# Windowed attention and a squared-ReLU layer: GpSimd's masks at another time, other first blocks and turns, a fourth relu tile

## The chip, the cores and the metric

The kernel runs on one core of a Trainium2 chip. The core has a matrix engine (TensorE, PE in the profile), VectorE (DVE), ScalarE (ACT), GpSimd (POOL) and SyncE (SP, which here issues the DMAs). The metric is the device time of one execution in microseconds; of several executions the median is given. A profiled execution gives the trace.

## The reference

Input are q, k and v of shape (8 batches, 8 heads, 576 positions, 64) in float32, two weights (512 x 2048 and 2048 x 512) and two scalars s and b. Output is (4608, 512) in float32.

```
scores = q @ k.T / 8, kept where |i - j| <= 32, else -1e9
attn   = softmax(scores);  x = (attn @ v), heads side by side: (4608, 512)
h = x @ w_in;  g = s * relu(h)**2 + b;  out = g @ w_out
```

## The kernel before

**Two halves on one engine.** PE does both the attention and the two weight products. A *block* is a run of tokens that goes through the first product together; the list `sizes` (L341) gives their lengths: 96, 256, 160, 256, 256 and then 512 each. The first three cover tokens 0 to 511. `s1(m, f0)` (L1108) does the first product of block m for a group of 128-wide slices of the hidden layer: four slices at once up to 128 tokens, two up to 256, one beyond (`group`, L1105). Its matmuls are L1119, into one of two halves of the PSUM tile W, taken in turn; ACT's relu (L1126) goes from there into one of NR1 tiles R1, taken in turn; DVE's square (L1128) goes into GT. `early()` (L1160) does the second product of the first 512 tokens, two slices at a time, into four PSUM banks (L1168), and DVE makes the result with s and b (L1153). `s2` (L1132) does the second product of all later tokens (L1137). For b, `colsum()` (L1176) sums w_out's columns on PE (L1182, L1189), with two helper tiles that GpSimd fills and that lie in the last two of the output tiles OUTS (L1180, L1181).

**Weights.** w_in and w_out come in four chunks of two halves each, through a ring of eight float32 tiles STG (512 KB loads, L550), and GpSimd casts each half to bf16 (L553, 128 x 1024). The loads are issued by SP in a fixed order; a load waits until its STG tile's earlier user has been cast. Batch 1's q and k pairs (256 KB loads, L662) follow w_out in the same ring.

**Attention of batches 0 and 1.** A *pair* is two heads of q or k. It is cast to bf16 (L687: for batch 1, q on GpSimd, k on DVE), and four PE transposes (L700) bring it into W, in one of the two halves in turn; ACT copies q from there (L705), DVE copies k (L706). A *turn* is q and k of one pair. `pair_scores` (L932) then does the scores (L939) and ACT the exponential (L982). In batch 0 the mask is in the scores' bank from the start (tile NEG, opened by L957); in batch 1 DVE multiplies with MASK (L987). A *unit* is 128 positions of attention output: L864 (times v), the reciprocal and the division on DVE (L888, L890), a transpose (L897), and ACT's copy into XT (L905), which the first product reads. Batch 0's units end at tokens 96, 224, 352, 480 and 576. v of batch 1 is cast by GpSimd, of later batches by DVE (L587).

**Attention of batches 2 to 7.** q and k are loaded in larger pieces (L747), cast (L755), transposed by DMAs that SP issues (L762), k is rearranged by GpSimd (L772); L783 clears margins of the q tile. Scores are L806, the exponential L834, the mask L838, with one of four tiles MASKS, of which the first is MASK.

**Masks.** `band` (L480) makes a tile with two GpSimd affine selects (L482, L487). IDENT and both halves of NEG are made at the start. `masks(after)` (L512) makes MASK's two halves, then three copies with parts cleared (L517, L520). It is called in `attention()` (L1050) with the last unit of batch 0 as `after`.

**The order of the work.** Each piece of work is added to a graph with an engine, an estimated cost, what it reads and writes, and a key. `plan()` (L127) goes through the graph with these estimates and always takes the piece that can start earliest, and of those with equal start the lowest key; that gives each engine's fixed order. `emit()` writes it with semaphore waits. An estimate decides the order alone, not the time on the chip. The order in which pieces are added matters too, as it sets the dependencies: two pieces in the same half of W follow each other as they were added. FIRST (L34) is the list by which the first three blocks' `s1` calls are added: (m, i) is block m with weight chunk i, and TURN adds one turn of batch 1. HELD (L38) is, for each chunk of w_out, the delay in ns that `plan()` assumes between its cast and its first reader. `due(c, u)` (L464) gives a unit's key from the blocks' planned times.

Of the kernel before, what the change touches and what calls it, by code (L numbers as in the profile page):

```python
# [19 lines left out]
NUNIT = (NTILE + 1) // 2  # L20
# [10 lines left out]
WINE = ("pool", "pool", "pool", "pool")  # L31
TURNKEY = -17.5
TURN = (None, 0)
FIRST = ((0, 0), (1, 0), (0, 1), (1, 1), (2, 0), (2, 1), (0, 2), (1, 2), (2, 2), TURN, (0, 3), TURN, (1, 3), TURN, (2, 3), TURN)  # L34
WOUTE = (("pool", "pool"),) * 4
TAIL = ("act", "dve")
HOST = (("k", 3), ("q", 0))
HELD = (2200.0, 1500.0, 1000.0, 1000.0)  # L38
OPEN = -24.4
REST = ("pool", "pool")  # L40
ORDER1 = (("w", 0), ("w", 1), ("w", 2), ("w", 3), ("p", 0), ("p", 1), ("p", 2), ("p", 3),
# [285 lines left out]
def bass_sliding_window_symmetric__then__act_starrelu_kernel(  # L327
# [10 lines left out]
    B = q.shape[0]  # L338
    T = B * S

    sizes = [96, 256, 160, 256, 256]  # L341
    NE = 3
    while sum(sizes) < T:
        sizes.append(min(512, T - sum(sizes)))
# [6 lines left out]
    with ExitStack() as es:  # L351
# [16 lines left out]
            uid["n"] += 1  # L368
            return es.enter_context(nc.psum_tensor(f"{nm}_{uid['n']}", list(shape), dt))

        NSTG, NNAT, NEX, NXN, NR1, NOUT, XR = 8, 6, 5, 5, 3, 5, 2048
        WIN_BF = sb((128, 4, DFF), BF16, "win")
        WOUT_BF = sb((128, 16, DM), BF16, "wout")
        XT = sb((128, NPAIR, XR), BF16, "xt")
# [14 lines left out]
        MASK = MASKS[0]  # L389
# [7 lines left out]
        ONESW = sb((128, 128), BF16, "onesw")  # L397
# [5 lines left out]
        OUTS = [sb((128, DM), F32, "outs") for _ in range(NOUT)]  # L403
# [17 lines left out]
        g = _Graph(queues)  # L421
        add = g.add
# [70 lines left out]
        band(IDENT[:, :], ONESW[:, :], "IDENT", 0, 0, -98)  # L493
        for p0 in (0, 64):
            band(NEG[p0:p0 + 64, :], NEG[p0:p0 + 64, :], ("NEG", p0), 0, 64, -97, -FAR, source=("NEG", p0))
        ones = ONESW.rearrange("p (one c) -> p one c", one=1).to_broadcast((128, 4, 128))
        add("pe", [lambda e: e.matmul(W[:, 1, :].rearrange("p (a c) -> p a c", a=4), lhsT=ONESW[:, :], rhs=ones,
                                      start=True, stop=True)] * WARM,
# [12 lines left out]

        def masks(after):  # L512

            for p0 in (0, 64):
                band(MASK[p0:p0 + 64, :], ONESW[p0:p0 + 64, :], ("MASK", 0, p0), 0, 64, -24.0, waits=[after])
            for i, cuts in ((1, ((0, 96), (64, 0))), (2, ((64, 96),)), (3, ((0, 0),))):
                add("pool", lambda e, i=i: e.tensor_copy(MASKS[i][:, :], MASK[:, :]), 250,  # L517
                    reads=[("MASK", 0, 0), ("MASK", 0, 64)], writes=[("MASK", i, 0), ("MASK", i, 64)], key=0.0)
                for p0, c0 in cuts:
                    add("pool", lambda e, i=i, p0=p0, c0=c0: e.memset(MASKS[i][p0:p0 + 64, c0:c0 + WIN], 0.0), 150,  # L520
                        writes=[("MASK", i, p0)], key=0.0)
        for i in range(2):
            for c0 in (0, WIN + S):
                zero("dve", QT[i][:, :, c0:c0 + WIN], ("QTZ", i, c0), 150, key=-98 if i == 0 else -20)
            add("dve", lambda e, i=i: e.memset(VB[:, i * NUNIT:i * NUNIT + NUNIT, :, :].rearrange("p t h c -> p (t h) c")[:, :, D:D + 1], 1.0), 150,
                writes=[("VBO", i)], key=-57 if i == 0 else -20)
# [3 lines left out]
        land = {}  # L530
# [53 lines left out]
        def cast_v(c, u, key, eng, slack):  # L584
            vs, vb, n = number(c, u) % NUNIT, number(c, u) % (2 * NUNIT), 64 * len(tiles(c, u))
            add(eng, (lambda e: e.copy(VB[0:n, vb, :, 0:D], VST[0:n, vs, :, :])) if eng == "act" else
                (lambda e: e.tensor_copy(VB[0:n, vb, :, 0:D], VST[0:n, vs, :, :])),  # L587
                {"act": 617.0, "dve": 420.0, "pool": 750.0}[eng],
                reads=[("VST", vs)], writes=[("V", vb, y) for y in (0, 1)], key=key, slack=slack)

        def load_rows(y, load_key):

# [426 lines left out]
        def attention():  # L1019
            seq = {"k": -200.0}  # L1020

            def nxt():
                seq["k"] += 1.0
                return seq["k"]

            def w(which, i):
                for x in (0, 1):
                    load_weights(which, i, x, nxt(), WINE[i] if which == "in" else WOUTE[i][x])

            for pr in range(NPAIR):  # L1030
                for name in "qk":
                    load_pair(0, name, pr, nxt())
                    turn_pair(0, name, pr, -60.0 + 0.1 * pr, banks, K0[pr] if name == "k" else Q0[pr], 200.0)
                pair_scores(0, pr)
            pick()
            for name, t in ORDER0:
                if name == "v":
                    load_tail(nxt())
                elif name == "r":
                    load_rows(t, nxt())  # L1040
                elif name == "e":
                    load_rest(0, nxt(), REST[0], -26.5, 200.0)
                else:
                    w("in", t)
            place_v()
            turn_rest(0, -23.9, banks)
            place_tail()
            last_scores(0)
            first_units()
            masks(land["av", 0, NUNIT - 1])  # L1050
            for i, src in enumerate((moe_s, moe_b)):
                add("sp", lambda e, i=i, src=src: e.dma_start(SROW[0:128:32, i:i + 1], src.partition_broadcast(4)),
                    600.0, writes=[("SROW", i)], dma=("l", 1, 15.0), key=nxt())
            add("dve", lambda e: e.stream_shuffle(SB128[:, :], SROW[:, :], [0] * 32), 150,
                reads=[("SROW", 0), ("SROW", 1)], writes=[("SB128", 0), ("SB128", 1)], key=P2[0] - 8.0, slack=500.0)
            for step in ORDER1:
                if step[0] == "w":
                    w("out", step[1])
                elif step[0] == "v":
                    load_v(1, step[1], nxt(), "sp", [land["rows", y] for y in (0, 1)])  # L1060
                    cast_v(1, step[1], due(1, 0) - 4.0 + step[1], EV1[step[1]], 800.0)
                elif step[0] == "e":
                    load_rest(1, nxt(), REST[1], due(1, 0) - 1.4, 500.0)
                else:
                    for name in "qk":
                        load_pair(1, name, step[1], nxt())
            yield S
            for pr in range(NPAIR):
                if pr:
                    yield S  # L1070
                for name in "qk":
                    turn_pair(1, name, pr, TURNKEY + 0.1 * pr, banks, "dve" if name == "k" else "pool", 500.0)
                pair_scores(1, pr)
            turn_rest(1, due(1, 0) - 1.4, banks)
            last_scores(1)
            for u in range(NUNIT):
                last.append((1, u))
                close()
                yield closed[0]
            for b in range(PAIRS, B):  # L1080
                c = seq_of(b)
                later(b, due(c, group_of(b)[0]) - 24.0)
                for i, u in enumerate(group_of(b)):
                    load_v(c, u, due(c, u) - 35.0, late(b), [paced(b, PACEV[min(b, 4) - 2][i])])
                    cast_v(c, u, due(c, u) - 4.0, EV2[i], SLACK[3])
                for u in group_of(b):
                    unit(c, u)
                    yield closed[0]
            if seq_tiles(LONG) % 2 == 0:
                unit(LONG, seq_units(LONG) - 1)  # L1090
            while last:
                close()
            yield T
# [81 lines left out]

        def colsum():  # L1176

            even, block = OUTS[NOUT - 2][:, 0:128], OUTS[NOUT - 1][:, :]
            made = [land["av", 0, NUNIT - 1]]
            add("pool", lambda e: e.memset(even, 1.0 / 32), 150, writes=[("OUTS", NOUT - 2)], key=-19.0, waits=made)  # L1180
            add("pool", lambda e: e.memset(block, 0.0), 500, writes=[("OUTS", NOUT - 1)], key=-19.0, waits=made)  # L1181
            add("pe", [lambda e, fc=fc, x=x: e.matmul(  # L1182
                SC[32 * x:32 * x + 32, 0, 0:128], lhsT=ONESW[:, 0:32], rhs=WOUT_BF[:, fc, 128 * x:128 * x + 128],
                start=(fc == 0), stop=(fc == 15)) for fc in range(16) for x in range(4)],
                1100, reads=["ONESW"] + [("Wout", i, x) for i in range(4) for x in (0, 1)], writes=[("SC", 0)], key=-12.0)
            add("dve", [lambda e, x=x: e.tensor_copy(block[32 * x:32 * x + 32, 128 * x:128 * x + 128],
                                                     SC[32 * x:32 * x + 32, 0, 0:128]) for x in range(4)],
                800, reads=[("SC", 0)], writes=[("OUTS", NOUT - 1)], key=-12.0)
            add("pe", lambda e: e.matmul(SC[:, 1, :], lhsT=even, rhs=block, start=True, stop=True),  # L1189
                950, reads=[("OUTS", NOUT - 2), ("OUTS", NOUT - 1)], writes=[("SC", 1)], key=-12.0)  # L1190
            add("dve", lambda e: e.tensor_scalar(CVEC[:, :], SC[:, 1, :], SB128[:, 1:2], None, ALU.mult),
                680, reads=[("SC", 1), ("SB128", 1)], writes=[("CVEC", x) for x in (0, 1)], key=P2[0])

        units, made = attention(), 0
# [6 lines left out]
        made = next(units)  # L1201
        colsum()
        for m, i in FIRST:
            if m is None:
                made = next(units)
# [268 lines left out]
```

## Time and profile before

| | us |
|---|---|
| median of 3 executions | 316.41 (315.55 to 317.66) |
| the profiled execution | 318.05 |
| its span, first to last instruction | 316.3 |
| PE busy | 303.9 (96%) |
| DVE, ACT, POOL busy | 194.8, 141.9, 91.7 |
| mean granted PE clock | 0.987 |

The profile's page has a row of tenths for each engine over 40 equal slices of 7.9 us: 9 means busy for 90% or more. PE's row is 9 from the eleventh slice on; the first ten have smaller digits. The row PEclk is the clock granted to PE in tenths of full speed. DMA was busy for 73% of the span; its busiest slices moved 380 to 393 GB/s, from 16 to 36 us, when the weights come in.

| stretch, us | PE busy | DVE busy | ACT busy | POOL busy | clock | GB/s |
|---|---|---|---|---|---|---|
| 0 to 20 | 15.93 | 10.75 | 11.73 | 7.73 | 0.91 | 295 |
| 20 to 40 | 17.65 | 11.30 | 9.02 | 17.64 | 1.00 | 371 |
| 40 to 60 | 18.01 | 13.54 | 9.39 | 10.46 | 0.91 | 245 |
| 60 to 72 | 11.40 | 11.54 | 4.60 | 9.65 | 1.00 | 168 |
| 80 to 100 | 20.00 | 16.22 | 9.66 | 6.97 | 1.00 | 189 |

A matmul's end is modelled, so a busy PE can still have small losses. A wait is put down to what came last.

### The profile page before, as it was taken

How to read it: one execution, taken by the hardware profiler on the slowest of the kernel's cores; microseconds unless marked ns; L12 is line 12 of the kernel's file. 1: busy time of each engine (PE TensorE's matmuls, PEld its weight loads, DVE VectorE, ACT ScalarE, POOL GpSimd, SP SyncE). 2: the span in 40 equal slices, each digit the busy share in tenths (PEclk: the TensorE clock that was granted, in tenths of full speed). 3: DMA queues.
4: the chain of work that ended last, by engine and by line, in shares of the span. 5: the costliest groups of instructions: out<-in, count | busy, mean ns of one | idle time of the engine just before them, and what ended most of it. 6: DMA issues, size and time to landing. Idle time of an engine off the chain costs nothing.

```text
span 316.3 us, 7961 instructions
## 1 busy us (share of the span) xinstructions
PE 303.9 (96%) x3348; PEld 161.6 (51%) x3348; DVE 194.8 (62%) x387; ACT 141.9 (45%) x224; POOL 91.7 (29%) x110
## 2 busy tenths in 40 slices
PE   6888969999999999999999999999999999999995
PEld 2466656567664454544444444444444444444444
DVE  4666465895897897795577576967445543333312
ACT  4746326356544775654265435444444333333300
POOL 3468973670406136131513411451000000000000
PEclk9799979999999999999999999999999999999999
DMA  6999999998994998799799799996221110000022
GB/s 214 330 380 388 360 229 241 225 188 296 248 182 137 297 166 164 242 206 153 184 290 151 149 251 313 167 169 157 64 63 51 52 46 33 35 35 33 36 96 74
DMA packets 100055, 56.10 MB, mean 177 GB/s; under 512 B 72048, under 2 KB 91248, under 8 KB 100016
## 3 DMA queue, kind: packets, MB, share of 16 engines
q1 hardware_dynamic: 100016, 55.56, 73.0%
q8 instruction: 27, 0.44, 0.6%
q14 instruction: 12, 0.10, 0.1%
HBM read 36.70 MB, written 9.44 MB: 146 GB/s over the span
## 4 chain that ended last, share of the span: by engine, by line
PE 83%; DMA 5%; POOL 4%; SPq 3%; DVE 3%; issue 1%; POOLq 0%
PE w L1119 36%; PE o L1137 35%; PE avn L864 4%; DMA stg<-in_moe_w_in_dram 4%; POOL wout L553 3%; PE sc L806 2%; DMA stg<-in_v_dram 1%; PE avn L1168 1%; SPq L662 1%; PE o L1168 1%; DVE outs L1153 1%; PE w L700 1%; PE avn L897 1%; SPq L673 1%; DVE vb L587 1%
## 5 line engine op out<-in xcount | busy, mean ns | idle before, releaser
L1119 PE MATMUL w<-xt,win 128*128 128x512 bf16 (+3 forms) x768 | 144.8, 327 | 1.1 <-issue 0.6
L1126 ACT ACTIVATE r<-w 128x512 bf16<-128x512 f32 (+2 forms) x148 | 86.6, 586 | 104.0 <-PE w L1119 87.6
L1137 PE MATMUL o<-wout,gt 128*128 128x512 bf16 (+1 forms) x528 | 126.8, 373 | 0.3 <-DVE gt L1128 0.3
L1128 DVE TENSOR_TENSOR gt<-r 128x512 bf16<-128x512 bf16 (+2 forms) x148 | 77.2, 526 | 75.9 <-ACT r L1126 75.5
L1119 PEld LDWEIGHTS w<-xt,win 128*128 128x128 bf16 x768 | 67.7, 98 | 53.9 <-issue 0.8
L1137 PEld LDWEIGHTS o<-wout,gt 128*128 128x128 bf16 x528 | 50.7, 98 | 55.8 <-DVE gt L1128 0.6
L755 POOL CAST nat<-stg 128x1024 bf16<-128x1024 f32 (+1 forms) x21 | 26.6, 1265 | 64.4 <-DMA stg<-in_q_dram 42.5
L772 POOL COPY kt<-ktr 128x512 bf16<-128x512 bf16 (+1 forms) x30 | 31.1, 1037 | 37.4 <-DMA ktr<-nat 35.9
L834 ACT ACTIVATE ex<-sc 128x1024 bf16<-128x1024 f32 (+1 forms) x28 | 28.6, 1023 | 22.5 <-PE avn L864 21.7
L1153 DVE SCALAR_TENSOR_TENSOR outs<-o,sb,cvec 128x512 f32<-128x512 f32 (+1 forms) x35 | 25.4, 728 | 11.4 <-PE o L1137 11.3
L890 DVE TENSOR_TENSOR xn<-avn,rec 128x512 bf16<-128x512 f32 (+1 forms) x31 | 21.3, 688 | 1.0 <-DVE rec L888 0.2
L838 DVE TENSOR_TENSOR ex<-ex,mask 128x1024 bf16<-128x1024 bf16 (+1 forms) x28 | 21.2, 757 | 1.1 <-ACT ex L834 0.5
L864 PE MATMUL avn<-vb,ex 64*64 64x65 bf16 x944 | 19.9, 197 | 0.3
L864 PEld LDWEIGHTS avn<-vb,ex 64*64 64x64 bf16 x944 | 12.9, 106 | 13.2 <-issue 7.8
L755 DVE CAST nat<-stg 128x1024 bf16<-128x1024 f32 (+1 forms) x15 | 12.2, 810 | 3.7 <-DMA stg<-in_k_dram 1.9
L587 DVE CAST vb<-vst 128x512 bf16<-128x512 f32 (+1 forms) x28 | 13.8, 494 | 0.8 <-DMA vst<-in_v_dram 0.7
L888 DVE RECIPROCAL rec<-avn 128x8 f32<-128x8 f32 (+1 forms) x31 | 6.2, 201 | 8.3 <-PE avn L864 8.0
L806 PE MATMUL sc<-qt,kt 64*64 64x128 bf16 x432 | 11.3, 216 | 0.0
L700 PE MATMUL w<-ident,nat 128*128 128x128 bf16 x64 | 7.0, 253 | 3.9 <-POOL nat L687 3.4
L905 ACT COPY xt<-avn 128x512 bf16<-128x512 bf16 (+2 forms) x14 | 7.1, 516 | 6.3 <-PE avn L897 6.3
L705 ACT COPY qt<-w 128x512 bf16<-128x512 bf16 x8 | 4.7, 584 | 11.3 <-PE w L700 11.3
L553 POOL CAST win<-stg 128x1024 bf16<-128x1024 f32 x8 | 8.6, 1080 | 3.6 <-DMA stg<-in_moe_w_in_dram 3.4
(119 smaller groups left out, 156.8 us busy)
## 6 DMA issues: line engine op xcount, KB each, us to landing
out_dram<-outs SPq DMA_DIRECT2D x35, 256.0 KB, 2.6
vst<-in_v_dram SPq DMA_DIRECT2D x28, 256.0 KB, 4.4
stg<-in_k_dram SPq DMA_DIRECT2D x6, 1024.0 KB, 10.6
stg<-in_q_dram SPq DMA_DIRECT2D x6, 1024.0 KB, 6.4
stg<-in_moe_w_in_dram SPq DMA_DIRECT2D x8, 512.0 KB, 9.3
stg<-in_moe_w_out_dram SPq DMA_DIRECT2D x8, 512.0 KB, 10.3
stg<-in_q_dram SPq DMA_DIRECT2D x8, 256.0 KB, 5.3
stg<-in_k_dram SPq DMA_DIRECT2D x8, 256.0 KB, 5.1
```

Source lines behind the costliest of these rows:

```text
L553: add(eng, (lambda e: e.copy(dst, stg)) if eng == "act" else (lambda e: e.tensor_copy(dst, stg)), {"act": 1040.0, "dve": 690.0, "pool": 11 ...
L755: add(eng, lambda e, x=x: e.tensor_copy(nat[0:top, 1024 * x:1024 * x + 1024].rearrange("p (i h d) -> p h i d", h=H, i=2), stg[0:top, :].re ...
L772: add("pool", lambda e, c=c, w=w: e.tensor_copy(KT[slot][:, :, c:c + w].rearrange("p a (s i) -> p a s i", i=4), KTR[slot][:, :, :, c // 4: ...
L834: add("act", lambda e, dst=flat_dst, src=flat_src: e.activation(dst, src, AF.Exp, bias=0.0, scale=0.125), 190 + 0.833 * 512 * len(hs), rea ...
L838: add("dve", lambda e, flat=flat, mask=mask: e.tensor_tensor(flat, flat, mask, ALU.mult), 130 + 0.53 * 512 * len(hs), reads=[("E", ei, hp, ...
L864: return [lambda e: e.matmul(av[64 * x:64 * x + 64, h, 0:D + 1], lhsT=buf[64 * g:64 * g + 64, h % 2, h // 2, c:c + 64], rhs=VB[64 * g:64 * ...
L890: add("dve", lambda e: e.tensor_tensor(XN[xi][0:p1, :].rearrange("p (a c) -> p a c", a=H), av[0:p1, :, 0:D], REC[ri][0:p1, :].rearrange("p ...
L1119: add("pe", [lambda e, g=g, kc=kc: e.matmul(wt[:, g, :], lhsT=WIN_BF[:, kc, (f0 + g) * 128:(f0 + g + 1) * 128], rhs=XT[:, kc, t0 % XR:t0 % ...
L1126: add("act", lambda e: e.activation(rt, wt, AF.Relu, bias=0.0, scale=1.0), 190 + 0.833 * ng * nt, reads=[("W", wb)], writes=[("R1", rb)], ...
L1128: add("dve", lambda e: e.tensor_tensor(GT[gs][:, f0:f0 + ng, g0:g0 + nt], rt, rt, ALU.mult), 130 + 0.53 * ng * nt, reads=[("R1", rb)], wri ...
L1137: add("pe", [lambda e, fc=fc: e.matmul(O[:, ob, 0:cn], lhsT=GT[gs][:, fc, g0:g0 + 128], rhs=WOUT_BF[:, fc, c0:c0 + cn], start=(fc == 0), s ...
L1153: add("dve", lambda e: e.scalar_tensor_tensor(OUTS[us][:, 0:cn], bank, SB128[:, 0:1], CVEC[:, c0:c0 + cn], ALU.mult, ALU.add), 200 + 1.07 ...
```

## The change

Six edits.

1. MASK's two halves are made at the start, behind NEG, with key -96 and no wait for batch 0's attention. The two fills for `colsum()` follow them, waiting only for the last of these selects.
2. The three copies of MASK and their clearings wait for the last V cast of batch 1 (the new entry `land["vb", 1]`).
3. The first blocks are 224, 128 and 160 tokens.
4. FIRST has another order: chunk 1 of block 0 directly behind chunk 0, chunk 3 of block 0 ahead of the first turn, and the first two turns directly behind each other.
5. HELD is 1500 for chunks 2 and 3 of w_out.
6. There are four R1 tiles instead of three.

```
-FIRST = ((0, 0), (1, 0), (0, 1), (1, 1), (2, 0), (2, 1), (0, 2), (1, 2), (2, 2), TURN, (0, 3), TURN, (1, 3), TURN, (2, 3), TURN)
+FIRST = ((0, 0), (0, 1), (1, 0), (1, 1), (2, 0), (0, 2), (2, 1), (1, 2), (2, 2), (0, 3), TURN, TURN, (1, 3), TURN, (2, 3), TURN)
-HELD = (2200.0, 1500.0, 1000.0, 1000.0)
+HELD = (2200.0, 1500.0, 1500.0, 1500.0)
...
-    sizes = [96, 256, 160, 256, 256]
+    sizes = [224, 128, 160, 256, 256]
...
-        NSTG, NNAT, NEX, NXN, NR1, NOUT, XR = 8, 6, 5, 5, 3, 5, 2048
+        NSTG, NNAT, NEX, NXN, NR1, NOUT, XR = 8, 6, 5, 5, 4, 5, 2048
...
+        for p0 in (0, 64):
+            band(MASK[p0:p0 + 64, :], ONESW[p0:p0 + 64, :], ("MASK", 0, p0), 0, 64, -96)
+        even, block = OUTS[NOUT - 2][:, 0:128], OUTS[NOUT - 1][:, :]
+        add("pool", lambda e: e.memset(even, 1.0 / 32), 150, writes=[("OUTS", NOUT - 2)], key=-95.0, waits=[g.tasks[-1]])
+        add("pool", lambda e: e.memset(block, 0.0), 500, writes=[("OUTS", NOUT - 1)], key=-95.0, waits=[g.tasks[-1]])
...
-            for p0 in (0, 64):
-                band(MASK[p0:p0 + 64, :], ONESW[p0:p0 + 64, :], ("MASK", 0, p0), 0, 64, -24.0, waits=[after])
             for i, cuts in ((1, ((0, 96), (64, 0))), (2, ((64, 96),)), (3, ((0, 0),))):
                 add("pool", lambda e, i=i: e.tensor_copy(MASKS[i][:, :], MASK[:, :]), 250,
-                    reads=[("MASK", 0, 0), ("MASK", 0, 64)], writes=[("MASK", i, 0), ("MASK", i, 64)], key=0.0)
+                    reads=[("MASK", 0, 0), ("MASK", 0, 64)], writes=[("MASK", i, 0), ("MASK", i, 64)], key=0.0, waits=[after])
...
+            land["vb", c] = g.tasks[-1]
...
-            masks(land["av", 0, NUNIT - 1])
...
+            masks(land["vb", 1])
...
-            even, block = OUTS[NOUT - 2][:, 0:128], OUTS[NOUT - 1][:, :]
-            made = [land["av", 0, NUNIT - 1]]
-            add("pool", lambda e: e.memset(even, 1.0 / 32), 150, writes=[("OUTS", NOUT - 2)], key=-19.0, waits=made)
-            add("pool", lambda e: e.memset(block, 0.0), 500, writes=[("OUTS", NOUT - 1)], key=-19.0, waits=made)
```

## The prediction

> **What bounds the kernel now.** I read the busy table, then the 40 slices, then PE's waits, then the timelines around the one large hole. PE is the bound from 76 us on: the slices show it full, and no wait of PE ends there. What this change can move lies in front, where PE holes show as digits under 9.
>
> ```profile
> PE 303.9 (96%) x3348; PEld 161.6 (51%) x3348; DVE 194.8 (62%) x387; ACT 141.9 (45%) x224; POOL 91.7 (29%) x110
> PE   6888969999999999999999999999999999999995
> POOL 3468973670406136131513411451000000000000
> PEclk9799979999999999999999999999999999999999
> ```
>
> The largest wait of PE is for POOL's cast of batch 1's first q pair (L687). Columns: total us, times, longest.
>
> ```profile
> PE w L700 <- POOL nat L687: 3.4, 2, 2.4
> PE w L497 <- DVE onesw L475: 1.1, 1, 1.1
> PE o L1168 <- POOL wout L553: 0.7, 1, 0.7
> PE w L1119 <- issue: 0.6, 1, 0.6
> ```
>
> The timelines of PE and POOL (start, length, what) show that hole and what POOL did instead.
>
> ```profile
> 38.54 1.03 PE L1168 MATMUL o<-wout,gt 128*128 128x512 bf16 x4
> 41.99 0.99 PE L700 MATMUL w<-ident,nat 128*128 128x128 bf16 x8 [2.42 <-POOL nat L687]
> 42.90 1.90 PE L1182 MATMUL sc<-wout,onesw 128*32 128x128 bf16 x64
> 44.73 0.61 PE L700 MATMUL w<-ident,nat 128*128 128x128 bf16 x4
> ...
> 37.23 1.04 POOL L553 CAST wout<-stg 128x1024 bf16<-128x1024 f32 x1
> 38.33 0.29 POOL L520 MEMSET mask<- 64x32 bf16 x2
> 38.69 1.04 POOL L553 CAST wout<-stg 128x1024 bf16<-128x1024 f32 x1
> 39.79 0.29 POOL L517 COPY mask<-mask 128x128 bf16<-128x128 bf16 x1
> 40.14 1.04 POOL L553 CAST wout<-stg 128x1024 bf16<-128x1024 f32 x1
> 41.24 0.68 POOL L687 CAST nat<-stg 128x512 bf16<-128x512 f32 x1
> ```
>
> Mask work stands between the w_out casts, the q cast comes last, and PE idles 2.42 us. The clock is granted in stretches of 3.4 us; the one after the hole is at half (columns: length, busy by engine, clock, DMA share, GB/s).
>
> ```profile
> 38.70:42.10 3.40, 0.98 (x6) 0.31 (x5) 1.25 (x1) 0.00 (x0) 3.15 (x5) 1.00 0.79 241
> 42.10:45.50 3.40, 3.40 (x81) 3.01 (x80) 1.96 (x5) 0.71 (x2) 2.27 (x6) 0.50 0.97 230
> 60.00:72.00 12.00, 11.40 (x191) 7.57 (x191) 11.54 (x21) 4.60 (x9) 9.65 (x10) 1.00 1.04 168
> ```
>
> **1. Masks made at the start.** Four band selects and two memsets move in front of POOL's first cast. The six selects already there run from 1.13 to 3.51 us, one per 0.43; so 4 x 0.43 + 0.20 + 0.52 + two gaps of 0.07 = 2.6 us, to 6.1. POOL is idle from 3.51 until 6.76 (q's landing), so 0.65 us of cover stays: cost 0. Past the cover, each us would delay batch 0's second q pair, whose transposes wait at 7.42. A select may slip in front of NEG's last one and hold PE's first opening matmuls (3.57) by 0.43; pair 1 has 1.0 us of idle PE ahead of it to absorb that.
>
> **2. POOL's casts of w_out.** Between 24.4 and 41.2 us the mask work is 0.29 + 0.35 + 0.36 + 0.29 + 0.20 + 0.52 + 0.36 + 0.29 + 0.29 = 2.95 us. Not all of it is gained, since the casts then run into their loads. The trace has the w_out landings at 29.36, 30.71, 32.01, 33.37, 36.08, 37.45 and 38.87 us (one is missing), one per 1.36, against 1.04 for a cast. The last cast starts at 40.14; it could start at 38.9, a gain of 1.2. The q pair landed at 39.57, so its cast runs from 40.0 to 40.6, and L700 can start at about 40.7 instead of 42.0. The k cast on DVE waits for a load as well (40.18) and does not move. SP issues batch 1's pairs when w_out casts free their tiles, so those issues come up to 1.2 us sooner; but these pairs land at one per 0.68 us up to 44.4, at some 380 GB/s, as much as the load stream shows anywhere, so I count nothing for them. V and batch 2's loads behind them in SP's queue may start 1 us earlier; nothing either.
>
> **3. Turns and blocks.** (0,3), two calls of 8 matmuls, now stands ahead of the first turn. Starts of successive matmuls are 43 ns apart at 96 columns, 69 at 160, 109 at 256: 0.42 ns a column and 2.5 ns. So 224 columns take 96 ns and (0,3) 1.5 us. PE leaves its last piece at 39.4 to 39.6; with (0,3) it has work until 41.0, past 40.7. The 2.42 hole closes; I leave 0.1 for the k half: **-2.3 us**. Bounds: -1.2 (only the earlier cast counts, because a piece of L1168 that stood before the turn moves behind it) and -2.42. The total of matmul columns is the same: 64 x (43 + 109 + 69) against 64 x (96 + 56 + 69) is 14.1 us both times, and 20 relu groups stay 20. Block 0 now needs unit 1's columns, copied at 19.35 to 19.94; the first group waited for a w_in cast until 20.23 anyway: 0.
>
> **4. The half clock.** With the hole gone, the stretch from 42.1 should run at full clock. Its price by rows: the 8 transposes took 0.99 us, and four take 0.22 at full (-0.55); L1182's 64 have no row at full clock (0 to -0.92); the rest is -0.1 to -0.25. Bounds 0 and -1.7 (half of 3.4); I take **-1.2**, nearest to the rows. The Trainium skill, TensorE: Matmul & The Clock Gate, What's actually happening, has the clock fall after at least one idle window of about 3.4 us; this trace shows it after 2.42 us of idle, so the measurement decides. By that rule this term would be 0 and the sum 1.7.
>
> **5. The three mask copies and four memsets** (3 x 0.29 + 4 x 0.12 with gaps, 1.8 us) follow batch 1's last V cast, which ends at 52.1. POOL then idles 3.01 us for a load of batch 2, so they cost 0. If that load came at once, they would delay batch 2's casts by 1.8; its scores start at 77.6, its first k copies are done by 70, so this is covered too. The added wait has only batch 2's casts behind it. The masks other than the first are read from batch 3 on.
>
> **6. Fourth relu tile, later due times for w_out chunks 2 and 3.** One wait of ACT for DVE is seen ahead of 75 us (0.38 at 34.17). The due times change only the order in which PE meets its work. 0, bounds -0.4 and +0.5.
>
> **7. What is late next.** DVE was busy 11.54 of 12 us from 60 to 72. Arriving 3.5 us sooner, the work of 40 to 72 (13.5 + 11.5 us) must fit into 28.5: 88%. I give back PE's own idle of that stretch, 12.0 - 11.4: **+0.6** (bounds 0 and +2.0, three result tiles of L1153 in a row). The loads for batches 3 and on are issued as PE and DVE proceed; batch 3's first k copy is done at 97.7, its scores start at 101.1: 3.4 us of slack, more than the gain.
>
> **Sum.** -2.3 - 1.2 + 0.6 = -2.9 us, from the profiled execution's 318.05 (span 316.3 and 1.75 around it) to 315.15. That execution lies 1.6 above the median of 316.41; the same difference on the median gives **313.5 us**. About 1% is what a measurement can tell from no change, so this is near the border.
>
> **Rivals.**
> - *Early stage gains too* (17%). Blocks 0 and 1 need three units instead of four, so chunks 0 and 1 can be done sooner, and PE's idle at 25.2 (0.62) and 30.2 (0.74) would go. For: both lie between such groups. Against: the first is not a wait for data. 2.4 + 1.7 + 1.4 - 0.6 = 4.9: 311.5.
> - *The clock term is nothing* (13%). The stretches begin at multiples of 3.4 us, so the hole may fall across two of them in ordinary executions, with no half clock to win. -2.3 + 0.6 = -1.7: 314.7. The clock rule cited above would give the same.
> - *The landings hold everything* (10%). PE comes to the turn with no more work than before, since early pieces of the second layer slipped behind it; 1.2 is left, minus 0.6: 315.8. This is also the case in which moving the masks does not shorten POOL's way.
> - *Slower: doubled turn* (18%). Two turns now stand in a row on two W banks. q0 must wait for the relu of (0,3)'s last group (0.6 + 0.3), q1 and k1 for the copies of q0 and k0 (0.58 and 0.69 plus 0.2 to 0.3 each). Before, (0,3) stood between. If the written order puts nothing of L1168 or L1182 there, PE idles 0.9 + 0.8 + 0.8 = 2.5 us, and a second stretch goes to half clock, +1.7: 4.2, and 0.5 of item 6, against the 1.2 of the cast: 3.5 slower, 319.9. It decides once less than some 1.5 us of other work stands between. Against: at 42.9 a 1.9 us piece stands right behind the first turn, and 44 of L1168's 64 matmuls (9.5 us) are still to come.
>
> **Numbers.** The forecast's case has 42%, 312.4 to 314.8; somewhat under half of it lies beyond 1% (313.25). Faster by over 1%: 0.20 + 0.17 = 0.37. Within: 0.22 + 0.13 + 0.10 = 0.45. Slower by over 1%: 0.18, the doubled turn. The range leaves that case out and takes the early gain in: 311.0 to 318.6; the likeliest case's own is 312.4 to 314.8.
>
> **What would show it.** POOL's w_out casts each start right behind a landing, the last near 38.9; the q cast ends near 40.7; two groups of L1119 at 224 columns stand ahead of L700; no half-clock stretch follows; POOL's copies lie in the idle time after 52; PE's hole at 60 to 70 stays below 1.5 us. A hole of over 1 us between the first two turns, or a wait of batch 2's or 3's scores for k copies, would make the prediction wrong.

## The result, and the profile after

| | kernel before | kernel after |
|---|---|---|
| median, us (22 executions each) | 317.49 | 315.97 |
| lowest to highest | 315.3 to 319.2 | 313.83 to 319.07 |
| profiled execution, its span | 318.05, 316.3 | 315.73, 313.9 |

The ratio is 0.995, with a 95% interval of 0.9931 to 0.9969: 1.5 us faster, where 2.9 had been forecast. The median of 316.41, from which the forecast of 313.5 was counted, came from three executions; the kernel before has 317.49 here and 317.25 to 317.37 in the four sets of the experiments (35, 34, 34 and 23 executions). So of the 2.5 us between 313.5 and 315.97, 1.1 is that base and 1.4 the effect itself. Ratios, and the averages further down, leave out the few executions that took over 1.5% longer than the fastest of the same kernel; medians keep them.

The profiled executions stand further apart (2.3 us by time, 2.4 by span). The page of the kernel after, in the rows that were shown of before: busy time with share and instructions, then busy tenths of 40 slices.

```profile
PE 295.9 (94%) x3304; PEld 160.5 (51%) x3348; DVE 195.9 (62%) x387; ACT 142.1 (45%) x224; POOL 90.8 (29%) x110
PE   6788979999998999999999999999999999999996
POOL 5367765780226136120613331341000000000000
PEclk9999999999999999999999999999999999999999
```

Of PE's matmuls 44 have no record here (3304 against 3348 weight loads), so its lower sum is no gain. PEclk has no slice under 9 any more; before, two were. PE's first ten slices are still not full. The wait for w_out (L1172), 1.2 at 30.97 us, stands where the kernel before had holes of 0.62 and 0.74, at 25.2 and 30.2. PE's waits (total us, times, longest):

```profile
PE w L704 <- DVE nat L691: 2.2, 2, 1.5
...
PE o L1172 <- POOL wout L556: 1.2, 1, 1.2
...
PE avn L901 <- DVE xn L894: 0.7, 1, 0.7
```

Lines between L500 and L1175 are three or four higher than before: L704 is the former L700 (transposes of q and k), L691 their cast, L1172 the second product of the first 512 tokens, L556 the weight casts, L590 the V casts, L759 the casts of later batches. The first turn waits again, now for DVE's cast of k. PE, DVE and POOL around it (start, length, what):

```profile
38.42 0.93 PE L1123 MATMUL w<-xt,win 128*128 128x224 bf16 x8
39.19 0.59 PE L1172 MATMUL avn<-wout,gt 128*128 128x512 bf16 x2
41.28 0.40 PE L704 MATMUL w<-ident,nat 128*128 128x128 bf16 x4 [1.50 <-DVE nat L691]
41.60 1.08 PE L1182 MATMUL sc<-wout,onesw 128*32 128x128 bf16 x64
```

```profile
40.63 0.59 DVE L691 CAST nat<-stg 128x512 bf16<-128x512 f32 x1 [1.62 <-DMA stg<-in_k_dram]
```

```profile
39.22 1.04 POOL L556 CAST wout<-stg 128x1024 bf16<-128x1024 f32 x1 [0.39 <-DMA stg<-in_moe_w_out_dram]
40.33 0.61 POOL L691 CAST nat<-stg 128x512 bf16<-128x512 f32 x1
```

POOL's casts now wait for their loads, as item 2 had it: the last starts 0.05 us behind its landing at 39.17, and q is cast at 40.94. But PE has nothing to do from 39.78 on, and the turn begins with its k half, whose load landed at 40.61. The hole of 2.42 has become one of 1.50, not of 0.1. L1182 runs at full clock: 1.08 us, 1.90 before.

Where the time went, by the starts of five pieces of work, in the first trace of each kernel and in a second one (us):

| | before | after | change | before, second | after, second | change |
|---|---|---|---|---|---|---|
| first turn | 41.99 | 41.28 | -0.71 | 41.67 | 40.70 | -0.97 |
| from there to batch 1's last scores | 15.92 | 14.11 | -1.81 | 15.78 | 14.16 | -1.62 |
| to block 3's first product | 7.48 | 7.38 | -0.10 | 7.48 | 7.38 | -0.10 |
| to batch 2's first scores | 12.25 | 11.81 | -0.44 | 12.26 | 11.88 | -0.38 |
| to the end | 238.67 | 239.32 | +0.65 | 238.83 | 240.67 | +1.84 |
| sum: span | 316.31 | 313.90 | -2.41 | 316.02 | 314.79 | -1.23 |

The turn starts 0.7 to 1.0 sooner. The stretch behind it is 1.6 to 1.8 shorter, of which 0.67 is work that lies elsewhere now (16 matmuls at 96 columns and 16 at 256 less, 16 at 128 and four of L1172 more: 0.69 + 1.74 - 0.90 - 0.86) and the rest, 1.0 to 1.1, the clock, less what the doubled turn costs. The kernel with the masks alone (below) has PE's order of before and full clock, so it prices the clock by itself: from the turn to the fourth piece behind it, L1168 (there L1172), it is 4.00 and 3.86 us in the two traces of before and 2.53 there, 1.3 to 1.5 less. Of the 3.1 us that PE is ahead at batch 2's scores, 0.65 and 1.84 are lost again behind them.

The landing of k differs by some tenths between executions and moves all that follows. Counted from that landing, batch 2's first scores come 37.5 and 37.4 us later in the two traces of before, 34.0 and 34.1 in those of after, and 34.0 in that of the masks alone. So in the traces the front is some 3.4 us shorter, and the masks alone bring all of it.

### The profile page after: what moved, and what is told of

It is laid out like the page before. It is cut to its first block, busy times and chain, and to the rows that moved or that the text cites. A ratio compares the mean times of both kernels' runs of the same rounds, so it can differ in the third digit from the quotient of the medians.

```text
span 313.9 us, 7901 instructions
## 1 busy us (share of the span) xinstructions
PE 295.9 (94%) x3304; PEld 160.5 (51%) x3348; DVE 195.9 (62%) x387; ACT 142.1 (45%) x224; POOL 90.8 (29%) x110
## 4 chain that ended last, share of the span: by engine, by line
PE 81%; DMA 10%; DVE 3%; issue 3%; POOL 1%; SPq 1%; ACT 0%; POOLq 0%
PE w L1123 35%; PE o L1141 35%; PE avn L868 4%; DMA stg<-in_moe_w_out_dram 3%; DMA stg<-in_moe_w_in_dram 3%; DMA stg<-in_k_dram 2%; DMA stg<-in_q_dram 2%; PE sc L810 2%; PE avn L1172 2%; PE o L1172 1%; DVE gt L1132 1%; SPq L666 1%; PE avn L901 1%; PE sc L943 0%; DVE kt L710 0%
## 5 line engine op out<-in xcount | busy, mean ns | idle before, releaser
L1123 PE MATMUL w<-xt,win 128*128 128x512 bf16 (+4 forms) x749 | 140.2, 324 | 3.0 <-ACT r L1130 1.4
L1141 PE MATMUL o<-wout,gt 128*128 128x512 bf16 (+1 forms) x510 | 123.1, 372 | 2.0 <-issue 1.4
L759 POOL CAST nat<-stg 128x1024 bf16<-128x1024 f32 (+1 forms) x21 | 24.9, 1186 | 62.6 <-DMA stg<-in_q_dram 39.7
L842 DVE TENSOR_TENSOR ex<-ex,mask 128x1024 bf16<-128x1024 bf16 (+1 forms) x28 | 22.4, 801 | 1.0 <-ACT ex L838 0.2
L759 DVE CAST nat<-stg 128x1024 bf16<-128x1024 f32 (+1 forms) x15 | 12.7, 849 | 4.6 <-DMA stg<-in_q_dram 2.4
L590 DVE CAST vb<-vst 128x512 bf16<-128x512 f32 (+1 forms) x28 | 13.9, 501 | 0.8 <-DMA vst<-in_v_dram 0.8
L704 PE MATMUL w<-ident,nat 128*128 128x128 bf16 x64 | 6.5, 232 | 3.7 <-DVE nat L691 2.2
L556 POOL CAST win<-stg 128x1024 bf16<-128x1024 f32 x8 | 8.5, 1057 | 3.9 <-DMA stg<-in_moe_w_in_dram 3.7
L1172 PE MATMUL avn<-wout,gt 128*128 128x512 bf16 x30 | 8.9, 380 | 0.3 <-issue 0.3
```

The lines of the kernel that those rows point to most:

```text
L759: add(eng, lambda e, x=x: e.tensor_copy(nat[0:top, 1024 * x:1024 * x + 1024].rearrange("p (i h d) -> p h i d", h=H, i=2), stg[0:top, :].re ...
L842: add("dve", lambda e, flat=flat, mask=mask: e.tensor_tensor(flat, flat, mask, ALU.mult), 130 + 0.53 * 512 * len(hs), reads=[("E", ei, hp, ...
L1123: add("pe", [lambda e, g=g, kc=kc: e.matmul(wt[:, g, :], lhsT=WIN_BF[:, kc, (f0 + g) * 128:(f0 + g + 1) * 128], rhs=XT[:, kc, t0 % XR:t0 % ...
L1141: add("pe", [lambda e, fc=fc: e.matmul(O[:, ob, 0:cn], lhsT=GT[gs][:, fc, g0:g0 + 128], rhs=WOUT_BF[:, fc, c0:c0 + cn], start=(fc == 0), s ...
L1172: add("pe", [lambda e, fc=fc, bank=bank, gs=gs, g0=g0: e.matmul(bank, lhsT=GT[gs][:, fc, g0:g0 + 128], rhs=WOUT_BF[:, fc, :], start=(fc == ...
```

## The experiments

Every kernel was timed beside the kernel before in five rounds. Theory at the outset: the masks' way out of POOL's weight casts brings the turn 1.2 us nearer to its loads and with that the clock; blocks and turns bring little.

**The kernel before once more**, to see what a measurement without any change gives.

> The kernel before, unchanged, to see the granted clock of many executions. Theory 1 (the half-clock stretch after the 2.4 us hole is part of nearly every execution): mean granted clock of most executions at 0.985 to 0.992, and the trace has a half-clock stretch that begins within 3.4 us of the hole. Theory 2 (the profiled execution was a special case, the 3.4 us stretches fall anywhere): more than half of the executions at 0.994 or above, with no stretch at half clock behind the hole. Both: ratio 1.000 within 0.003.

0.9987 (0.9961 to 1.0013), median 316.88. Its trace has the hole again, 2.44 us, with a stretch at half clock behind it.

**The masks alone.**

```diff
 kernel before
+ edits 1 and 2 (masks at the start, copies behind batch 1's last V cast)
```

> The kernel before with edits 1 and 2 alone: mask halves and fills at the start, mask copies behind the last V cast. Blocks, turns, due times and relu tiles as before. Theory 1 (landings hold): POOL's w_out casts each wait for their load, the last one starts 1.0 us sooner, and the first turn starts at 41.2 to 41.4, because the k pair's landing and its cast on DVE now come last; hole 1.6 to 2.0 us; ratio 0.997, by 0.7 us plus part of the clock. Rival (moving the masks is the whole gain): the ratio of the changed kernel, 0.995. Rival (no gain without more work ahead of the turn): 0.999 to 1.000.

0.9936 (0.9909 to 0.9964), median 315.30: all of the change's gain. The hole is 1.71 us, and the clock does not fall. PE in that trace:

```profile
41.09 0.68 PE L704 MATMUL w<-ident,nat 128*128 128x128 bf16 x8 [1.71 <-POOL nat L691]
41.70 1.08 PE L1182 MATMUL sc<-wout,onesw 128*32 128x128 bf16 x64
```

The turn starts 0.4 us behind the landing of k, against 1.8 in the kernel before and 0.67 after. It begins with its q half there, and what ends the hole is GpSimd's cast of q, done at 41.04 behind the last cast of w_out; that one started 0.05 behind its landing.

**Blocks and turns alone.**

```diff
 kernel before
+ edits 3 and 4 (first blocks 224, 128, 160; the new FIRST)
```

> The kernel before with edits 3 and 4 alone: blocks of 224, 128, 160 and the new order of turns; masks between the casts as before, three relu tiles. Theory 1: the q cast still ends near 41.9, so the first turn starts at 41.9 or later, but with the two groups of block 0's chunk 3 done ahead of it: 0.6 to 1.5 us gained, no half-clock stretch; ratio 0.996. Rival (doubled turn): PE idles between the turns, over 1.5 us in total from 42 to 50; ratio 1.003 or more.

1.001 (0.9982 to 1.0038): nothing. PE in that trace:

```profile
40.78 1.08 PE L1182 MATMUL sc<-wout,onesw 128*32 128x128 bf16 x64 [1.52 <-POOL wout L553]
41.79 0.62 PE L700 MATMUL w<-ident,nat 128*128 128x128 bf16 x8
...
44.32 0.40 PE L700 MATMUL w<-ident,nat 128*128 128x128 bf16 x4 [0.39 <-DVE kt L706]
```

L1182 has gone ahead of the turn and waits 1.52 for the last cast of w_out. The doubled turn costs one wait of 0.39 us. The clock stayed full in this trace, and counted from the landing of k batch 2's first scores come after 34.4 us, 3.0 sooner than before; but 1.7 of these are lost behind them (240.4 us from there to the end, 238.7 before). So the new order gets at the same hole as the masks, and in the medians nothing of it is left.

**Edits 1 to 4, without the due times and the fourth relu tile**, in two sets of runs.

```diff
 kernel after
- HELD 1500 for chunks 2 and 3; NR1 = 4
+ HELD 1000 for chunks 2 and 3; NR1 = 3
```

> The changed kernel without edits 5 and 6: due times and three relu tiles as before. Theory 1 (only the masks matter): as with the masks alone, ratio 0.993 to 0.996. Rival (blocks and turns need the later due times and the fourth relu tile): 0.997 or more. Rival (edits 5 and 6 cost something): 0.991 to 0.993.

> The kernel before with edits 1 to 4 once more, beside the others of this chip. Theory (edits 5 and 6 bring nothing, since one wait of 0.38 us for a relu tile was all that was seen): 0.993 to 0.996, not told apart from the kernel after. Rival (the order that edits 5 and 6 bring about costs 0.002): 0.993 again and a mean granted clock as in the kernel after.

0.993 (0.9904 to 0.9956) and 0.9934 (0.9902 to 0.9967). The medians, 314.95 and 315.70, lie around that of the masks alone. The kernel after is nominally 0.002 above both; the intervals overlap, so this is not shown. The traces show what edits 5 and 6 change: without them L1182 stands ahead of the first turn, and the hole is 0.64 and 0.70 instead of 1.50 and 1.38. PE in the second trace:

```profile
38.74 1.08 PE L1182 MATMUL sc<-wout,onesw 128*32 128x128 bf16 x64 [0.70 <-POOL wout L556]
39.75 0.62 PE L704 MATMUL w<-ident,nat 128*128 128x128 bf16 x8
...
42.45 1.12 PE L1189 MATMUL sc<-outs 128*128 128x512 f32 x2 [0.56 <-DVE outs L1186]
```

The turn starts 0.65 and 0.66 behind the landing of k, as after, and PE waits a little later for DVE's copies of the sums (1.36 and 0.56). Counted from k's landing batch 2's first scores come after 34.5 and 33.8 us. So a shorter hole alone is no gain, where only other work has been put into it.

**The kernel after once more.**

> The changed kernel once more, beside the three others of this call, for a second trace and more granted clocks. Theory 1 (the gain is mostly the clock): three quarters of the executions or more at a clock of 0.998 or above, against about a quarter of the kernel before; the executions at that clock within 0.5 us of the kernel before's at that clock (315.7 against 316.0); ratio 0.995. The 0.7 us wait of PE for a division on DVE near 101 us comes again if PE's lead itself causes it; it is gone if it was chance. Rival (the gain is the shorter hole): at equal clock it is still 1.2 us or more faster.

0.9957 (0.9922 to 0.9992), median 315.45. The hole ahead of the turn is 1.38.

**The hole filled with idle matmuls**, first in the kernel before, then in the one with the masks alone.

```diff
 for m, i in FIRST:
     if m is None and it is the first turn:
+        add("pe", 8 (with the masks alone: 7) matmuls of ONESW, 128 x 512, into half 1 of W, cost 0, key -17.6)
```

> The kernel before with eight idle matmuls (ones, 128 x 512, 1.7 us) on PE directly ahead of the second layer's last pieces before the first turn; nothing reads them, the order of everything else is the same. It prices the clock alone: the turn can start no sooner than before. Theory 1 (clock term 1.2 us in nearly every execution): mean clock 0.994 and above, and 0.9 to 1.5 us faster, ratio 0.996. Theory 2 (half clock is rare in ordinary executions): ratio 0.999 to 1.002.

> The kernel before with edits 1 and 2, and seven idle matmuls (ones, 128 x 512, 1.5 us) on PE ahead of the last pieces before the first turn; nothing reads them. Theory 1: the hole of 1.7 us falls to 0.3, all executions at 0.998 or above, and 0.2 to 0.5 us faster than with the masks alone on average: ratio 0.992. Rival (the masks alone already hold the clock; PE's idle matmuls only delay its next pieces): 0.994 to 0.996.

In the kernel before: 0.9977 (0.9947 to 1.0007), median 316.23. The hole falls to 0.69 and the clock stays full behind it, in the trace:

```profile
40.89 0.62 PE L700 MATMUL w<-ident,nat 128*128 128x128 bf16 x8 [0.69 <-POOL nat L687]
41.44 1.08 PE L1182 MATMUL sc<-wout,onesw 128*32 128x128 bf16 x64
```

The span is 313.9, as after, though no real work was moved, and that trace's loads were early (last half of w_out 37.7, before 38.9). The sign is that of item 4, but the interval reaches 1. On top of the masks the filler gave 0.9999 (0.9969 to 1.0028): the masks' gain is gone. In its trace nothing idles from 40 to 60 us, but w_out's last half landed at 40.9 only, and k at 42.21; the turn started 0.47 behind that, at 42.68, as soon as q was cast (42.62). So in that trace the late loads held it and not the filler. Why its other executions are late too is not settled.

**k's load moved forward.** Theory by then: the turn hangs on the landing of k.

```diff
-ORDER1 = (("w", 0), ("w", 1), ("w", 2), ("w", 3), ("p", 0), ...
+ORDER1 = (("w", 0), ("w", 1), ("w", 2), ("p", 0), ("w", 3), ...
```

> The changed kernel, with batch 1's first q and k pair loaded ahead of w_out's last chunk instead of behind it. Theory (the k pair's landing at 40.6 us holds the first turn): the pair lands 2.7 us sooner, near 37.9, the first turn starts at or before 40.0 and the hole of 1.5 us is gone; w_out's last chunk lands 1.4 us later; by the turn alone 0.5 to 1.2 us faster than the changed kernel, ratio 0.991 to 0.994. Rival (what is late next takes it: w_out's last chunk, the sum over w_out and the second layer's last pieces, or DVE from 60 us): ratio 0.995 or more, with a new hole at one of these.

1.0026 (0.9997 to 1.0055). It didn't answer: k landed at 39.5, but `plan()` put the first turn behind other work, at 46.52 us. Later in its trace:

```profile
64.54 0.40 PE L901 MATMUL sc<-ident,xn 128*128 128x128 bf16 x4 [1.89 <-DVE xn L894]
```

A hole of 1.89 us at 64.5 is followed by a half stretch from 66.1. The question needed a kernel with the same order on every engine.

**A shorter last load of w_out**, which leaves every order as it is.

```diff
-            add("sp", lambda e: e.dma_start(stg, src), ...
+            add("sp", lambda e: e.dma_start(stg[:, 0:1, 0:256], src[:, 0:1, 0:256]), ...   # for the last half chunk alone
```

> The kernel after, with the order of every engine unchanged, but the last half chunk of w_out is loaded by a quarter only (128 of 512 KB; its other values are left from an earlier tenant of the tile, so three quarters of that half chunk count wrongly in the second layer). That takes about 1.0 us of the 1.36 between landings out of the load stream ahead of batch 1's first q and k. Theory (the landing of batch 1's k, cast on DVE, holds the first turn once the masks are gone from GpSimd): k lands some 1.0 us sooner, the turn starts 0.6 to 0.7 us behind it as before, PE's hole ahead of it falls from 1.5 (1.38 in the second trace) to 0.3 to 0.7, and the median falls by 0.7 to 1.0: 314.5, ratio about 0.991. Rival (PE's own order or GpSimd's cast of w_out holds it; then the load does not matter): the hole stays above 1.2 and the ratio at 0.995. Rival two (what is won there is lost to the late loads of batch 3): the hole falls, the stalls between 89 and 105 us grow by as much, the ratio stays at 0.995.

0.9917 (0.9889 to 0.9945), median 314.82, as the first theory had it, though this interval and that of the kernel after (0.9931 to 0.9969) overlap. PE and DVE in that trace (lines again four higher):

```profile
40.01 0.40 PE L708 MATMUL w<-ident,nat 128*128 128x128 bf16 x4 [0.35 <-DVE nat L695]
```

```profile
39.24 0.71 DVE L695 CAST nat<-stg 128x512 bf16<-128x512 f32 x1 [0.57 <-DMA stg<-in_k_dram]
```

k landed at 39.22, the turn started 0.79 behind it, and the hole fell from 1.50 to 0.35. The shortened half landed 0.41 us behind the one before it, against 1.43 in the kernel after. So what holds the turn in the kernel after is the load stream. This is the direct evidence on item 3. The shorter load brings w_out's last half, q and k sooner all together, and so doesn't tell them apart; in the traces of after it is k's cast that ends the hole.

**Where the gain is lost behind 77 us.** The trace of the kernel after has a stall at 102.1, the second one of 1.41 at 89.3. PE, then DVE, of the second:

```profile
89.29 0.32 PE L868 MATMUL avn<-vb,ex 64*64 64x65 bf16 x16 [1.41 <-issue]
```

```profile
87.06 0.69 DVE L759 CAST nat<-stg 128x1024 bf16<-128x1024 f32 x1 [1.99 <-DMA stg<-in_k_dram]
87.67 1.52 DVE L842 TENSOR_TENSOR ex<-ex,mask 128x1024 bf16<-128x1024 bf16 x1
```

DVE takes its work in the planned order: the cast waits 1.99 for batch 3's k, the mask multiply behind it comes late, and PE's attention output, which needs it, starts as it ends. The stall at 102.1 (0.71) is another: in that trace k landed at 85.57, its cast started at 85.59, and PE waits for a division that DVE does behind two squares of 1.2 us each. In the kernel before the same cast starts at 85.13 with no wait. The time from batch 2's first scores to the end is 238.7 and 238.8 in the two traces of before, 239.3 and 240.7 in those of after and 239.4 with the masks alone, so something is lost there in each. SyncE issues batch 3's q in both kernels at 74.04 (second trace of after 74.84), although PE is 3 us ahead. Its queue in the second trace of after (start, length, what):

```profile
64.97 4.51 SPq L766 DMA_TRANSPOSE qt<-nat  x2
69.52 1.54 SPq L766 DMA_TRANSPOSE ktr<-nat  x1
71.10 0.64 SPq L581 DMA_DIRECT2D vst<-in_v_dram  x1
71.79 2.96 SPq L1161 DMA_DIRECT2D out_dram<-outs  x4
74.84 0.52 SPq L751 DMA_DIRECT2D stg<-in_q_dram  x1
75.40 0.89 SPq L751 DMA_DIRECT2D stg<-in_k_dram  x1
```

Batch 2's transposes and the four result DMAs stand ahead of it without a gap. The first attempt moved these four to ScalarE:

```diff
-            put(sub, res, bank, 0, DM, P2[0] + 1.0)
+            put(sub, res, bank, 0, DM, P2[0] + 1.0, "act")
```

> The kernel after, but the four result DMAs of the first 512 tokens are issued by ScalarE and not by SyncE, so that they no longer stand ahead of batch 3's loads in SyncE's queue; the order around the first turn is the same, PE's order from block 3 on comes out different in places, since the plan is made again. Theory (SyncE's queue fixes when batch 3's k lands, and DVE's cast of it, taken in order, holds up the units of batch 2 that PE waits for at 89 to 105 us): batch 3's first loads are issued at 71 to 72 us and not at 74.0 to 74.8, its k lands at 82 to 84 and not at 85.6 to 87.0, PE's stalls between 80 and 110 fall from 0.7 (1.84 in the second trace) to below 0.3, and the median by 0.7 to 1.0: ratio about 0.992. Rival (DVE's long instructions beside GpSimd's copies make the stalls, not the landing): the issues come sooner, the stalls stay at 0.7 or more, ratio 0.995. Rival two (ScalarE is held up by waiting for the results, so its relu and copies come late): waits of PE for ACT appear between 68 and 76 us, ratio 0.997 or above.

> The kernel before with edits 1 to 4 (masks at the start, new blocks and order of the turns, but three relu tiles and the old due times), and the four result DMAs of the first 512 tokens on ScalarE. Theory (the two gains add up): 0.993 for the first, less 0.002 for the second: 0.991, median about 314.4. Rival (nothing hangs on SyncE's queue): 0.993. If it is ScalarE that is held up: 0.995 or above.

1.0031 (0.9996 to 1.0066) and 1.0008 (0.9976 to 1.004). The loads did not go out sooner but later, at 76.14. There is a second hold in the code: batch 3's loads are made to wait for the landing of batch 2's last V load (`piece`'s waits), and that V load was issued at 72.50 here, 70.56 in the kernel after. ScalarE spent 2.67 us on three of the issues, and its next relu ended an idle time of 2.28 us. So these two say only that ScalarE is no free place for them there; as a test of the queue they failed.

The next two take the wait away: in the kernel after, with the four result DMAs left out too, and in the kernel with edits 1 to 4 with everything computed, where one of the four still stands ahead of the loads:

```diff
-  ([land["v", seq_of(b - 1), group_of(b - 1)[-1]]] if b > PAIRS or ...
+  ([land["v", seq_of(b - 1), group_of(b - 1)[-1]]] if b > PAIRS + 1 or ...
```

> The kernel after, with batch 3's loads no longer made to wait for batch 2's last V load, and without the four result DMAs of the first 512 tokens (rows 0 to 511 of the output are not written). Theory (SyncE's queue sets when batch 3's k lands, and that makes the stalls): batch 3's loads are issued at 71 to 72 us and not at 74.0 to 74.8, k lands 2 to 3 us sooner, at 82 to 83, PE's stalls between 80 and 110 us fall from 0.7 and 1.8 to below 0.3, ratio 0.991 to 0.993. Rival (the stalls come from VectorE's order and long instructions, wherever the loads land): the loads land sooner, stalls of 0.5 to 1.5 us stay, ratio 0.995.

> The kernel before with edits 1 to 4, and batch 3's loads without the wait for batch 2's last V load; everything is computed. SyncE then has one of the four result DMAs ahead of these loads and three behind. Theory (the queue makes the stalls): loads issued 1 to 2 us sooner than 74.1, stalls between 80 and 145 us below 0.4, ratio 0.990 to 0.992 against 0.993 without this. Rival (the stalls are of VectorE's order): 0.993, the stalls at other places.

The first has batch 3's loads at 71.39 and its k at 81.8 (85.57 and 87.03 before that). Its traced span is 312.9, the shortest of all, and from 60 to 150 us one wait of PE is left:

```profile
PE o L1141 <- DVE gt L1132: 0.2, 1, 0.2
```

That is as the theory has it, though the hole at the turn was 1.82 in that execution. Its ratio of 0.9944 (0.9918 to 0.9971) does not tell it from the kernel after. The second gave 0.9966 (0.9944 to 0.9988): k of batch 3 came at 80.81, and the next batch then waited. PE and DVE there:

```profile
115.51 1.04 PE L1141 MATMUL o<-wout,gt 128*128 128x512 bf16 x4 [0.98 <-DVE gt L1132]
```

```profile
111.81 0.69 DVE L759 CAST nat<-stg 128x1024 bf16<-128x1024 f32 x1 [1.83 <-DMA stg<-in_k_dram]
```

So the theory holds for the stall of 1.41 in the second trace of after, by one trace without it, and where everything is computed the remedy only moves it one batch on. What the stalls cost over many executions stays open.

## Why the prediction was wrong

**Item 1 (masks at the start, 0) and item 5 (copies in POOL's idle time, 0): right.** GpSimd was done with the masks and fills at 6.01 and then idled 1.18 us for q's load, so it paid nothing at the start; a select did slip in front of NEG's last one, and PE's first opening waited 0.5 for it. The copies and clearings lie at 53.2 to 55.7, behind the last V cast, and GpSimd then waited 1.41 for a load.

**Item 2 (casts run into their loads): right**, with 39.2 for the last cast where 38.9 was forecast, and 40.94 for the end of the q cast where 40.6 to 40.7 was forecast. The landing itself was 0.3 later in that execution.

**Item 3 (-2.3): this step failed.** It had two parts: a turn that starts 1.2 to 1.3 sooner, and a hole ahead of it that (0,3) fills. The first part came: 0.7 to 1.0 by the traces, and 1.1 to 1.2 against the landing of k (1.8 and 1.87 us behind it before, 0.67 and 0.64 after), which came 0.3 to 0.4 later in these executions. The second did not. PE was not busy until 41.0 but until 39.8, and 1.4 to 1.5 us of hole are left where 0.1 was forecast. 16 matmuls of L1168 stand ahead of the turn where there were 20, so of the 1.5 us of (0,3) 0.86 was exchange and 0.64 addition. So PE's holes ahead of the turn shrank by 0.9 to 1.1, where 2.3 was forecast. The lower bound came near the value, with the reason that it gave ("a piece of L1168 that stood before the turn moves behind it"), and the third rival with it. What the earlier casts bring, the masks bring without the blocks and turns: 34.0 us from k's landing to batch 2's scores with them alone, 34.0 and 34.1 after. By the medians of the runs the blocks and turns gave nothing: 1.001 alone, and with the masks no more than these alone. The shortened load shows what the rest of the hole was worth: 1.0 us less load, 1.0 to 1.15 less hole, ratio 0.9917.

**Item 4 (-1.2): right in its cause, wrong in how often.** An execution that has the half clock behind the hole pays 1.3 to 1.5 for it, as worked out under the table. But the kernel before does not have half clock in every execution. In 37 of 124 the mean granted clock is 0.998 or more; these take 316.47 on average, the other 87 take 317.53. Of the kernel after (two sets) 24 of 31 are at that clock, 315.57 against 316.70. So the clock is worth 1.06 x 87/124 - 1.13 x 7/31 = 0.74 - 0.26 = 0.5 us of the average, and the rest of the 1.4 between the averages (317.21 and 315.82) is what the full-clock executions show, 316.47 - 315.57 = 0.9, with some 0.5 either way by their scatter. The rival that counted the clock at nothing had named the reason, the phase of the stretches, but as all or none. Some of these stretches lie at the start (7.9 to 11.4 in the trace of before), so not all of the 0.74 belongs to the hole.

The Trainium skill (TensorE: Matmul & The Clock Gate, What's actually happening) calls the window free-running. The traces agree in that: the stretches begin at another time in each execution (38.7 and 38.0 for the one with the hole in the two traces of before). The section's full idle window of about 3.4 us is not needed: the clock fell behind holes of 2.42, 2.44 and 1.89 us, in steps of 3.4 us in which PE was busy for 0.99, 1.24 and 1.26 us.

**Item 6 (0): right** as far as the runs can tell (0.993 and 0.9934 without it, 0.995 and 0.9957 with it), though the order that it changed is the one at the hole: L1182 behind the first turn and not ahead of it.

**Item 7 (+0.6): within its bounds, wrong in place.** From 60 to 72 us nothing was given back: PE was busy 11.73 of 12 us there, 11.40 before. 0.65 and 1.84 were lost at 89 to 105 us, where the forecast saw 3.4 us of slack. It took the slack from batch 3's scores, which PE reaches at 101; but in DVE's order the cast of k stands ahead of a mask multiply of batch 2 that PE waits for at 89. "The loads for batches 3 and on are issued as PE and DVE proceed" was not so: SyncE's queue issued them at the same time as before.

**The slower rival, the doubled turn**, did not come: 0.39 us with blocks and turns alone, no hole over 0.16 between 42 and 60 us after. The 1.5 us of other work that it saw as the border were there: L1182's 1.08 and L1172's pieces were put between.

**The early stage** gained 0.1 to 0.2 by its holes and not the 1.4 of its rival: 0.62 and 0.74 became one of 1.20, and 0.98 became 0.85 in the second traces.

**The sum over executions**: -0.9 for the path and -0.5 for the clock, where -1.7 (-2.3 + 0.6) and -1.2 were forecast. The base of three executions took 1.1 us more off the absolute number; the 315.97 that came is next to the third rival's 315.8, but as a ratio the result lies halfway between that rival (0.998) and the forecast (0.991).

## What to carry to other kernels

Before a hole is counted as filled, list what stands ahead of it in the new order piece by piece: work that is only exchanged for other work fills nothing, and what ends the hole is the landing and the cast of its latest input. A price seen in one trace (here a stretch at half clock) is to be weighed by how many executions have it: the mean granted clock of each execution tells. When the front of a kernel becomes faster, look in the DMA-issuing queue for what does not follow, and in each engine's fixed order for what stands behind its first late load.

## What the runs showed that was not expected

**The load stream differs between executions.** The same loads in the same order end at other times: w_out's last half at 38.9 and 38.3 in the two traces of the kernel before, at 37.3 to 40.9 over the kernels whose loads up to there are alike and whole. In the late one a single w_in load landed 2.9 us behind its neighbour (24.43, 27.32), where 1.3 to 1.4 is the rule. This is as large as the whole effect under study.

**How long a hole must be for the clock to fall.** The granted clock changes in steps of 3.4 us, and where a step begins differs between executions. So a hole counts by what of it lies in one step. The holes of 1.38 to 1.71 kept full clock, but a border cut them (1.50 into 0.57 and 0.93). One of 1.82 (38.57 to 40.39) lay whole within one step (38.1 to 41.5), in which PE was busy for 1.59 us, and kept it. One of 1.89 (62.65 to 64.54) in a step of 62.7 to 66.1, with PE busy for 1.26, brought the half clock, and so did those of 2.42 and 2.44, with 0.99 and 1.24. Busy time is not all that counts: near the start, steps with 1.71, 1.79 and 1.97 us busy were followed by half clock in three traces, while steps with 1.70 and 1.79 in another trace were not; why stays open. An estimate from the holes: if 1.82 to 2.15 us of idle in one step (3.41 less 1.59 and 1.26) decide, a hole of 2.42 escapes only where a step's border cuts it into two parts both shorter than that, in 1.2 to 1.9 of 3.4 us of its phases or 36 to 55%. By the same estimate a hole of 1.5 doesn't suffice; 77% of the kernel after's executions are at full clock, and the rest would then be due to stretches near the start, as the traces of four other kernels have them at 7.9 to 8.7. 77% of 36 to 55% is 28 to 42%; 30% of the kernel before's executions are at full clock.
